# Attention and experts on one core: probabilities transposed in 32x32 blocks on VectorE, float32 products on eight tiles of the array, lists of tokens by comparisons

## The chip, the core and the metric

The kernel runs on one core of a Trainium2 chip. A core has a matrix engine (TensorE, PE in the profile; PEld is its loading of weights), a vector engine (VectorE, DVE), an engine for activations and copies (ScalarE, ACT), a general engine (GpSimd, POOL), and an engine that here only issues transfers (SyncE, SP). Each has its own queue of instructions, and semaphores hold an instruction until what it needs is there. Data live in HBM, in SBUF (128 partitions) and in PSUM, where the matrix engine writes (eight banks of 512 float32 a partition). The metric is the device time of one execution in microseconds.

## What is computed

Attention of 8 batches, each of 8 heads, 576 positions and 64 dimensions, with rotary positions; then a mixture of 8 experts over the 4608 tokens of 512 values, each token in the one expert that its gate puts first.

```python
q_rot, k_rot = (rotate(q), rotate(k))
scores = scale * np.matmul(q_rot, k_rot.transpose(0, 1, 3, 2))
scores = scores - np.max(scores, axis=-1, keepdims=True)
attn = np.exp(scores)
attn = attn / (np.sum(attn, axis=-1, keepdims=True) + 1e-09)
x = np.matmul(attn, v)                       # then [tokens, heads x dims]
...
logits = x @ w_gate
e_idx = np.argmax(logits, axis=1)            # gate_w: its softmax value
eom = 1.0 / (1.0 + np.exp(-(x @ w_output_gate)))
for e in range(E):
    mask = e_idx == e
    h = np.maximum(x[mask] @ w1[e], 0.0)     # 512 -> 1024
    out[mask] = gate_w[mask, None] * eom[mask, e, None] * (h @ w2[e])
```

## The kernel before

The attention runs over 32 pairs of heads (8 batches of 4 pairs), 9 steps a pair. A step is 128 queries of one head against all 576 keys; the middle one, step 4, holds the last 64 queries of both heads. `Attention.step` emits, for each step, the scores, the peak, the exponential, the transposes and the splits of earlier steps; a table of events (`CFG["events"]`) hangs all other work on a step number counted from the pair's first step, and may be negative (preparation) or over 8 (work that falls into the next pair's steps).

For precision, an operand is taken as a sum of two parts of 12 bits, each of the matrix engine's fast form of float32 (f32r). What happens to a pair:

- **Preparation.** One transfer brings q and k, already transposed and doubled for the rotation (L373). POOL multiplies (L383) and adds (L387), and makes the high part of k (L362) and the low parts of k, q and v (L368); ScalarE makes the high parts of q and v (L360). SP then stacks the high and low parts of one head on 128 partitions by transfers from SBUF to SBUF (`ks` L408, `qs` L427, `bd` L433).
- **Scores.** 4 products of 128x288 a step (L478), 6 at the middle step (L472), two PSUM banks a step, two steps in flight. VectorE takes the peak (L484), ScalarE the exponential with the row's sum (L496).
- **Transposes.** TensorE turns each step's probabilities in blocks of 128x128 (L517, and L535 and L538 for the last 64 keys): 41 a pair. ScalarE takes the high part out of PSUM (L457), VectorE the low one (L461).
- **Products with the values.** 40 a pair (L562), 320 or 256 columns, the result transposed. It is taken out by ScalarE or VectorE (L360, L362).
- **Back.** 10 float32 products a pair (L581, each two records in the trace) transpose it back, add the parts of v, and give the gates' logits; VectorE divides by the sums (L587, L589).

After a batch's fourth pair, `place` works out the gates and each token's place in the list of its expert: 18 small pieces, one a step, most on VectorE, and then five scatters of token numbers to a list in HBM (L691), issued by POOL. Each scatter writes the same list, and so waits until the one before has landed.

The experts take slots of 256 (or 128) tokens of one expert. POOL gathers the rows (L895), TensorE transposes them (L933), the first product (L961, L951) and the second (L989) follow, POOL scatters the result (L1001). All weights are split into two parts on ScalarE (L917) and VectorE or POOL (L919). The first slots use lists that are complete two batches before the end; the lists for the others need the last batch's scatters.

Of the kernel before, what the change touches and what calls it, by code (L numbers as in the profile page):

```python
# [20 lines left out]
NP = H // 2  # L21
# [7 lines left out]
XW = DM + 1  # L29
BIG = float(1 << 22)  # L30
SLOT = 256
CFG = {
    "L": 2, "LH": 2, "LL": 2, "order": "SP1TXH2L0", "trr": 5, "por": 5, "ra": "P", "rm": "P", "pm": 4, "pt": [2,
    1], "place": 18, "placek": 2, "kh": "P", "kl": "P", "qh": "A", "ql": "P", "vh": "A", "vl": "P", "dup": "A",
    "ac": "AVVV",
    "events": [
# [5 lines left out]
    ],  # L42
}

# columns of the table of constants
C_E8, C_MASK, C_TOK, C_EB, C_SL, C_II, C_TRI, C_ONE = range(8)
# [6 lines left out]
def slot_counts(nb):  # L53
    """Slots of 256 tokens of an expert that the first nb - 2 batches certainly fill; those that certainly get more than
    128 after these; and the most slots of 128 that the rest may need."""
    n0 = min(5, -(-((nb - 2) * S - E * (SLOT - 1)) // SLOT)) if nb > 2 else 0
    n0 = max(0, n0)
    T = nb * S - n0 * SLOT
    n2 = max(0, -(-(T - E * P) // SLOT))
    return n0, n2, (T + E * (P - 1)) // P - 2 * n2  # L60


def const_table(nb):
    """Constants that depend on the shapes alone: [128, n] float32, with the column ranges."""
    p = np.arange(P, dtype=np.float32)[:, None]
    ii = np.concatenate([np.eye(D), np.eye(D)], 0)
# [4 lines left out]
    mask[QR:, 2] = 0.0  # L71
    tok = p + 128.0 * np.array([0, 1, 4, 2, 3])[None, :]
    eb = np.tile(np.arange(E) * float(list_rows(nb)), (P, 1))
    sl = np.concatenate([p // 2, p], 1)
    parts = [e8, mask, tok, eb, sl, ii, tri, one]
# [4 lines left out]
def rope_table():  # L80
    """cos and signed sin, in the layout [pair of heads x D, 2, S]."""
# [9 lines left out]

def body(ctx, tc, nb, offs, qk, v, rope, cst, gates, w, out):
# [6 lines left out]
    # what lives to the end; what the preparation of a pair needs (right); what the rest of the attention needs  # L99
# [6 lines left out]
    ps_t = pool(ctx, "ps_t", 2, space=PSUM)  # L106
    ps_a = pool(ctx, "ps_a", 2, space=PSUM)
    ps_s = pool(scores, "ps_s", 2, space=PSUM)
    pools = px, px2, pa2, pp1, pp2, ps_s, ps_t, ps_a
    # the rows of x with their gates, and the list of each expert's tokens  # L110
    xd = dpool.tile([NT, XW], F32, name="xd")
    nl = E * list_rows(nb)
    lst = dpool.tile([nl, 1], F32, name="lst")
# [4 lines left out]
    o = offs[C_II]  # L118
# [3 lines left out]
    stage = pa2.tile([P, 2, S], F32, tag="pm", name="stage", bufs=CFG["pm"]).rearrange("p a b -> p (a b)")  # L122
# [3 lines left out]
    ii = cpool.tile([P, H, D + 16], F32, name="ii")  # L126
# [3 lines left out]
    zero, big = stage[:, nst:nst + 256], stage[:, nst + 256:nst + 256 + nl // P]  # L130
    nc.vector.memset(zero, 0.0)
    nc.vector.memset(big, BIG)
    nc.scalar.dma_start(out=ct, in_=cst[:, 0:o])
    nc.scalar.dma_start(out=stage[:, 0:nst], in_=cst[:, o:])
    nc.scalar.dma_start(out=ii[:, :, D:], in_=gates)

    def consts():
        nc.vector.tensor_copy(ii[:, :, 0:D], sc(C_II).unsqueeze(1).broadcast_to((P, H, D)))
        nc.vector.tensor_copy(trib, sc(C_TRI))
        nc.vector.tensor_copy(oneb, sc(C_ONE))  # L140
        nc.vector.memset(cnt, 0.0)
        nc.sync.dma_start(out=lst.rearrange("(p n) o -> p (n o)", p=P), in_=big)

    att = Attention(tc, nb, pools, cc, ident, ii, first, trib, oneb, cnt, zero, qk, v, xd, lst)
    n0 = slot_counts(nb)[0]
    moe = Moe(tc, nb, (px, px2, ps_t), cc, ident, cnt, w, xd, lst, out)
    # the first slots' tokens are known before the last two batches
    if n0:
        g = att.done(nb - 3) + 1
        for k, f in enumerate(pieces(moe.table0(), 14)):  # L150
            att.at(g + k, 2, f)
        att.at(att.done(nb - 2) - att.nplace + 22, 2, moe.fetch)
# [7 lines left out]
    for g in range(att.G, att.G + 4):  # L160
        att.step(g)
    scores.close()
    if not n0:
        att.rest(lambda g: True)
        main.close()
        moe.open_right(pool(ctx, "mr", 1, side="right", reuse_waits="tile"))
        left = []
    else:
        att.rest(lambda g: g <= att.G + 4)
        moe.begin1()  # L170
        att.rest(lambda g: True)
        main.close()
    moe.open_left(pool(ctx, "ml", 1, side="left", reuse_waits="tile"),
                  pool(ctx, "ps_m", 1, space=PSUM, reuse_waits="tile"))
    if n0:
        # the tables of the slots are worked out beside the scatters
        a, b, n = att.last, pieces(moe.table1(), 60), len(att.last) - 10
        left = a[:n] + [lambda f=f, g=g: (f(), g()) for f, g in zip(a[n:], b)] + b[10:]
# [9 lines left out]
def pieces(gen, n):  # L188
    """The (at most n) parts of a generator as functions, to be called in turn."""
# [3 lines left out]
class Attention:  # L193
    """The attention of all pairs of heads, emitted step by step."""

    def __init__(self, tc, nb, pools, cc, ident, ii, first, trib, oneb, cnt, zero, qk, v, xd, lst):
        nc = tc.nc
        px, px2, pa2, pp1, pp2, ps_s, ps_t, ps_a = pools
# [4 lines left out]
        def init(bd, z, rz, ac):  # L203
# [3 lines left out]
            nc.gpsimd.memset(ac[1][:, 2, QR:], 0.0)  # L207

        for i in range(2):
            o = (pp1.tile([P, 2, P], F32R, name=f"bd{i}"), px.tile([P, 2 * NCH], F32, name=f"z{i}"),  # L210
                 px.tile([P, 2 * NCH], F32, name=f"rz{i}"), [px.tile([P, NCH, P], F32, name=f"ac{h}_{i}") for h in range(2)])
            self.inits.append(lambda o=o: init(*o))
            own.append(o)
        lgp = px.tile([P, NCH, H, 16], F32, name="lgp")
        self.inits.append(lambda: nc.gpsimd.memset(lgp, 0.0))
# [6 lines left out]
        # pieces of work by the step (9 a pair) and the place in it at which they are emitted  # L222
# [5 lines left out]
        def newxb(b):  # L228
            xbs[b] = px2.tile([P, NCH, XW], F32, tag="xb", name=f"xb{b}")

        for n, pr in enumerate(self.pairs):
            g, b = 9 * n, n // NP
            fs = {"load": pr.load, "rot1": lambda pr=pr: pr.rot(1), "key": pr.key, "rot0": lambda pr=pr: pr.rot(0),
                  "query": pr.query, "loadv": pr.loadv, "value": pr.value, "den": pr.den,
                  "tr0": lambda pr=pr: pr.rem(0), "tr1": lambda pr=pr: pr.rem(1),
                  "lo0": lambda pr=pr: pr.remlow(0), "lo1": lambda pr=pr: pr.remlow(1)}
            for h in range(2):
                for a in range(2):
                    for k in range(2):
# [871 lines left out]
```

## Time and profile before

| what | value |
|---|---|
| time, median of 3 runs | 1231.0 us (1230.33 to 1232.42) |
| span of the profiled execution | 1253.2 us |
| first product of scores | at 15.0 us |
| last product with the values | at 717.8 us |
| last interval without a matrix product over 10 us | 793.2 to 823.3 us |
| first products of the experts | at 730.7 us |

The profiled execution's own time is not given apart from its span; the span is 1.8% above the median of the runs. In the lines below, a row of a timeline gives start, duration, engine, line, operation, output and inputs, shapes and count; "a group of a line" gives count, then busy time and the mean of one in ns, then the idle time of the engine before it. Matrix products overlap, so that the distance from start to start, not the duration, is what one of them takes.

### The profile page before, as it was taken

How to read it: one execution, taken by the hardware profiler on the slowest of the kernel's cores; microseconds unless marked ns; L12 is line 12 of the kernel's file. 1: busy time of each engine (PE TensorE's matmuls, PEld its weight loads, DVE VectorE, ACT ScalarE, POOL GpSimd, SP SyncE). 2: the span in 40 equal slices, each digit the busy share in tenths (PEclk: the TensorE clock that was granted, in tenths of full speed). 3: DMA queues.
4: the chain of work that ended last, by engine and by line, in shares of the span. 5: the costliest groups of instructions: out<-in, count | busy, mean ns of one | idle time of the engine just before them, and what ended most of it. 6: DMA issues, size and time to landing. Idle time of an engine off the chain costs nothing.

```text
span 1253.2 us, 22141 instructions
## 1 busy us (share of the span) xinstructions
PE 1094.3 (87%) x7603; PEld 1016.4 (81%) x7603; DVE 948.0 (76%) x1656; ACT 764.6 (61%) x1502; POOL 624.3 (50%) x412
## 2 busy tenths in 40 slices
PE   3999977988988869878888889379999999999997
PEld 2999877887978868868778889268898988989986
DVE  6899957978969859859789867246567776786784
ACT  3787755765756646746657654125467675776573
POOL 5777548567575575576475221122144363344242
PEclk9999988998988989999989989779999999999999
DMA  7866846847656756756756689757668878798791
GB/s 224 220 192 180 181 87 167 196 106 203 147 139 171 162 111 179 172 107 188 160 109 160 141 204 242 151 141 228 225 206 305 293 251 298 255 327 275 270 334 40
DMA packets 97395, 242.72 MB, mean 194 GB/s; under 512 B 27613, under 2 KB 28924, under 8 KB 93312
## 3 DMA queue, kind: packets, MB, share of 16 engines
q1 hardware_dynamic: 88032, 221.46, 64.1%
q0 software_dynamic: 7776, 18.94, 4.9%
q8 instruction: 64, 1.05, 0.4%
q10 hardware_dynamic: 1472, 0.85, 0.2%
q14 instruction: 51, 0.42, 0.1%
HBM read 168.66 MB, written 20.11 MB: 151 GB/s over the span
## 4 chain that ended last, share of the span: by engine, by line
PE 34%; POOL 25%; issue 22%; DMA 13%; DVE 2%; SPq 1%; ACT 1%; POOLq 0%; ACTq 0%; DVEq 0%
PE py L989 14%; POOL raw L383 11%; PE ph L961 11%; POOL raw L387 5%; PE ph L951 4%; DMA qs<-raw 3%; DMA lst<-tok,pi 3%; POOL raw L368 2%; POOL lst L691 2%; POOL kl L368 2%; DMA ks<-kh 2%; DMA xg<-xd,0idx 2%; PE mtp L933 1%; DMA ks<-kl 1%; POOL kh L362 1%
## 5 line engine op out<-in xcount | busy, mean ns | idle before, releaser
L919 DVE TENSOR_TENSOR wl<-wr,wh 128x1024 fp32r<-128x1024 f32 x183 | 254.3, 1402 | 51.6 <-ACT wh L917 50.2
L496 ACT ACTIVATE pm<-sc,m 128x576 f32<-128x576 f32 x288 | 214.8, 746 | 80.1 <-DVE m L484 75.3
L484 DVE TENSOR_REDUCE m<-sc 128x1 f32<-128x576 f32 x288 | 215.6, 749 | 60.0 <-PE sc L478 58.5
L478 PE MATMUL sc<-ks,qs 128*128 128x288 f32 x1024 | 202.8, 323 | 65.2 <-DMA qs<-raw 45.0
L457 ACT CAST pt<-tp 128x512 fp32r<-128x512 f32 x288 | 168.3, 584 | 128.1 <-PE tp L517 127.8
L461 DVE TENSOR_TENSOR pt<-tp,pt 128x512 fp32r<-128x512 f32 x288 | 196.8, 683 | 34.0 <-ACT pt L457 30.5
L478 PEld LDWEIGHTS sc<-ks,qs 128*128 128x128 f32 x1024 | 157.4, 201 | 79.5 <-issue 48.6
L917 ACT CAST wh<-wr 128x1024 fp32r<-128x1024 f32 x208 | 212.8, 1050 | 8.4 <-DMA wr<-in_w 8.4
L989 PE MATMUL py<-wh,ht 128*128 128x512 f32 x640 | 216.4, 403 | 0.0
L562 PE MATMUL acc<-pt,vs 128*128 128x256 f32 (+1 forms) x1024 | 192.2, 314 | 8.2 <-POOL vs L368 5.8
L517 PE MATMUL tp<-ident,pm 128*128 128x128 f32 x1152 | 183.2, 284 | 13.0 <-DVE pt L461 11.6
L383 POOL TENSOR_TENSOR raw<-raw,rt 128x1152 f32<-128x1152 f32 x62 | 164.2, 2649 | 10.0 <-DMA raw<-in_qk 8.6
L961 PE MATMUL ph<-xt,wh 128*128 128x256 f32 x896 | 161.6, 283 | 0.2 <-DVE ht L964 0.2
L517 PEld LDWEIGHTS tp<-ident,pm 128*128 128x128 f32 x1152 | 145.7, 147 | 17.7 <-DVE pt L461 11.6
L562 PEld LDWEIGHTS acc<-pt,vs 128*128 128x128 f32 x1024 | 148.8, 193 | 13.7 <-POOL vs L368 7.2
L989 PEld LDWEIGHTS py<-wh,ht 128*128 128x128 f32 x640 | 121.2, 189 | 25.0
L961 PEld LDWEIGHTS ph<-xt,wh 128*128 128x128 f32 x896 | 139.1, 190 | 1.8 <-DVE xt L936 0.6
L691 POOL DMA_INDIRECT lst<-tok,pi x40 | 41.5, 1036 | 198.1 <-DMA lst<-tok,pi 140.4
L989 PE MATMUL py<-wl,ht 128*128 128x512 f32 x320 | 126.2, 394 | 0.0
L961 PE MATMUL ph<-xt,wl 128*128 128x256 f32 x448 | 126.2, 282 | 0.0
L919 POOL TENSOR_TENSOR wl<-wr,wh 128x1024 fp32r<-128x1024 f32 x25 | 61.3, 2454 | 86.6 <-ACT wh L917 73.3
L581 PE MATMUL po<-ii,ac 128*128 128x80 f32 x640 | 86.3, 286 | 5.6 <-DVE lgp L589 5.6
(194 smaller groups left out, 1769.9 us busy)
## 6 DMA issues: line engine op xcount, KB each, us to landing
wr<-in_w SPq DMA_DIRECT2D x208, 512.0 KB, 5.3
raw<-in_qk SPq DMA_DIRECT2D x31, 1152.0 KB, 6.0
qs<-raw SPq DMA_DIRECT2D x124, 256.0 KB, 4.6
vraw<-in_v SPq DMA_DIRECT2D x32, 320.0 KB, 6.8
xd<-xb SPq DMA_DIRECT2D x16, 513.0 KB, 7.3
ks<-kh SPq DMA_DIRECT2D x32, 144.0 KB, 6.4
ks<-kl SPq DMA_DIRECT2D x32, 144.0 KB, 5.3
ks<-kh SPq DMA_DIRECT2D x32, 128.0 KB, 4.9
```

Source lines behind the costliest of these rows:

```text
L383: self.eng(eng).tensor_tensor(out=rv, in0=rv, in1=self.rt[:, 2 * t:2 * t + 2, x], op=ALU.mult)
L457: self.nc.scalar.copy(hi, src)
L461: self.nc.vector.tensor_tensor(out=lo, in0=src, in1=hi.bitcast(F32), op=ALU.subtract)
L478: nc.tensor.matmul(ps[:, a, :HS], self.qs[h][:, w, c * P:c * P + P], self.ks[h][:, a * HS:a * HS + HS], start=(w == 0), stop=(w == 1))
L484: nc.vector.tensor_reduce(self.m[i], ps[:, :, :HS], axis=AX.XY, op=ALU.max, negate=True)
L496: nc.scalar.activation(pe.rearrange("p (a b) -> p a b", a=2), self.ps[i][:, :, :HS], AF.Exp, bias=self.m[i], scale=1.0, accum_out=self.z[: ...
L517: nc.tensor.transpose(out=tp[:, k, :], in_=pe[:, k0 + k * P:k0 + k * P + P], identity=ident)
L562: nc.tensor.matmul(acc[:, 0:n], self.vs[:, 2 * k + h, :, :].rearrange("p a b -> p (a b)"), m, start=(i == 0), stop=(i == 9))
L917: self.nc.scalar.copy(wh, r)
L919: eng.tensor_tensor(out=wl, in0=r, in1=wh.bitcast(F32), op=ALU.subtract)
L961: nc.tensor.matmul(ph[:, f, :], st[:, dc, fs], mv[:, dc, :], start=(n == 0), stop=(n == 11))
L989: self.nc.tensor.matmul(py[h], st[:, f, hs], mv, start=(f == 0 and n == 0), stop=(f == 7 and n == 2))
```

## The change

**Scores.** The stacking transfers are gone. `kh`, `kl` and `q` stay as they are, the first head on partitions 0 to 63, the second on 64 to 127, and a step has 6 products over 64 rows instead of 4 over 128:

```diff
-            for w in range(2):
+            r = slice(h * D, h * D + D)
+            for n, (w, mov) in enumerate(((1, self.kh), (1, self.kl), (0, self.kh))):
                 for a in range(2):
-                    nc.tensor.matmul(ps[:, a, :HS], self.qs[h][:, w, c * P:c * P + P], self.ks[h][:, a * HS:a * HS + HS],
-                                     start=(w == 0), stop=(w == 1))
+                    nc.tensor.matmul(ps[:, a, :HS], self.q[r, w, c * P:c * P + P],
+                                     mov[r, a * HS:a * HS + HS], start=(n == 0), stop=(n == 2))
```

`bd` for the middle step is copied by ScalarE (`lasts`). High parts of k and q are made on ScalarE, low ones on POOL. q and k come in two transfers.

**Transposes.** One VectorE instruction turns the 32x32 blocks of a step's 128x576 probabilities, a step later, from SBUF to SBUF; the 41 transposes, the casts (L457) and the subtractions (L461) are gone:

```diff
+        self.nc.vector.transpose(out=self.pt[:, st[0] + 5 * st[1] if st else 4, :], in_=self.pc.pop(i))
```

**Products with the values.** After the block transposes, the 32 partitions `32a` hold 32 keys of block j for the queries whose number within a chunk lies in quarter a. So v is loaded four times, once on each 32 partitions (four transfers of 288 KB), and for each of 18 blocks of keys there are 8 float32 products of 32 rows by 64 columns of the array, one for each quarter of queries and each head, in one accumulator of four banks:

```diff
+        for a in range(4):
+            r = slice(32 * a, 32 * a + 32)
+            for h in range(2):
+                u, o, n = (0, 32, 4 + (a < 2)) if h == 0 else (5 - (a > 1), 32 - 32 * (a > 1), 4 + (a > 1))
+                nc.tensor.matmul(self.acc[h * D:h * D + D, a, o:o + 32 * n], self.v[r, h, j, :],
+                                 self.pt[r, u:u + n, 32 * j:32 * j + 32], start=(j == 0), stop=(j == NB - 1),
+                                 skip_group_check=True)
```

That is 144 products a pair (L503), emitted in four pieces of 40, 40, 32 and 32 at steps 12, 14, 16 and 17 (steps 3, 5, 7 and 8 of the next pair). Three copies on ScalarE take the result out, five float32 products of 160 columns (L518) at step 19 transpose it back into the same four banks, three VectorE and two ScalarE instructions divide.

On TensorE, at step 3 of the second pair, the order before has transposes and products between scores (tp: transposed probabilities in PSUM; acc: the accumulator; pt, vs: parts of probabilities and values):

```order
L517 MATMUL tp_5_8963<-ident,pm_2_8932 128x128 x4
L478 MATMUL sc_8_8971<-ks_31_8528,qs_31_8549 128x288 x4
L517 MATMUL tp_6_8978<-ident,pm_2_8932 128x128 x4
L562 MATMUL acc_31_8989<-pt_31_8805,vs_8851 128x320
L562 MATMUL acc_31_8989<-pt_31_8806,vs_8851 128x320
```

and now, with scores of one step, the piece of 40 begins:

```order
L463 MATMUL sc_3_327<-kh_181,q_213 128x288 x2
L463 MATMUL sc_3_327<-kl_182,q_213 128x288 x2
L463 MATMUL sc_3_327<-kh_181,q_213 128x288 x2
L503 MATMUL acc_338<-pt_140,v_232 64x160
L503 MATMUL acc_338<-pt_140,v_232 64x128
L503 MATMUL acc_338<-pt_140,v_232 64x160
L503 MATMUL acc_338<-pt_140,v_232 64x128 x2
L503 MATMUL acc_338<-pt_140,v_232 64x160
```

The full-size products (L562) of the order before are shown in the last pair, where a row of scores stands among them; the small ones now run without a score between for 40 in a row. Each of them is compiled to two loads of weights and two products on the same tile, one after the other, as each float32 product is.

**VectorE.** In steady steps before (m: the peak; pt: the low part; ac: taking out; xb, lgp: the division):

```order
L484 TENSOR_REDUCE m_3_6580<-sc_3_6575 128x1
L362 COPY ac_0_113<-acc_22_6582 128x256
L461 TENSOR_TENSOR pt_23_6547<-tp_1_6588,pt_23_6546 128x4x128
L362 COPY ac_0_112<-acc_22_6569 128x256
L484 TENSOR_REDUCE m_4_6619<-sc_4_6612 128x1
L461 TENSOR_TENSOR pt_23_6547<-tp_2_6621,pt_23_6546 128x4x128
```

and now:

```order
L469 TENSOR_REDUCE m_5_9426<-sc_5_9419 128x1
L484 STREAM_TRANSPOSE pt_9266<-pm_4_9411 128x576
L469 TENSOR_REDUCE m_6_9489<-sc_6_9482 128x1
L484 STREAM_TRANSPOSE pt_9266<-pm_5_9428 128x576
L781 CAST 0ri<-0row 128x1
L469 TENSOR_REDUCE m_7_9505<-sc_7_9498 128x1
```

The transpose of one step stands behind the peak of the next, where the subtraction stood behind a transpose of TensorE and a cast of ScalarE.

**Lists.** `place` has 38 pieces; its small operations are on POOL (on VectorE for the last batch). A token's place in the lists is split into a row and a column; VectorE compares row numbers (128x288, five times), POOL column numbers times the token's number (128x128, five times, L676), five products of 128x288 (L684) add both up to an array of all lists in SBUF, and it is written to HBM once for the first slots and once for the rest. No scatter is left on POOL:

```order
L691 DMA lst<-tok_1869,pi_1976 36864x1
L383 TENSOR_TENSOR raw_1998<-raw_1998,rt 128x1152
L387 TENSOR_TENSOR raw_1998<-raw_1998 128x576
L691 DMA lst<-tok_1869,pi_1976 36864x1
L383 TENSOR_TENSOR raw_1998<-raw_1998,rt 128x1152
```

is POOL's order of before, between the rotations of a pair (raw: q and k with their rotation); now the same engine has

```order
L412 TENSOR_TENSOR raw_4570<-raw_4570,rt 128x1152
L621 COPY xb_3004<-eg_4595 128x5
L416 TENSOR_TENSOR raw_4570<-raw_4570 128x576
L676 TENSOR_SCALAR pl_4909<-row,lo_4815,tok_4821 128x128 x2
L394 TENSOR_TENSOR kl_4935<-raw_4570,kh_4934 128x576
```

where the comparisons stand between the rotations, and wait for VectorE and POOL alone.

```diff
+        nc.vector.tensor_scalar(T["ro"][:, c, :], row, T["hr"][:, c:c + 1], 0.0, op0=ALU.is_equal, op1=ALU.add,
+                                accum_out=T["no"][:, c:c + 1])
+        nc.gpsimd.tensor_scalar(T["pl"][:, c, :], row[:, 0:P], T["lo"][:, c:c + 1], T["tok"][:, c:c + 1], op0=ALU.is_equal,
+                                op1=ALU.mult)
...
+            nc.tensor.matmul(T["ls"], T["pl"][0:m, c, :], T["ro"][0:m, c, :], start=(c == 0), stop=(c == 4), skip_group_check=True)
```

**The end of the attention.** The first slot's rows are transposed, and its first 48 products (L991) emitted, between the last piece of products with the values and the back products; the last batch's `place` runs beside the first slots, two pieces for each part of a slot.

```diff
+            att.rest(lambda g: g <= att.G + 1)
+            for u in range(3):
+                moe.split(u)
+            att.rest(lambda g: g <= att.G + 8)
+            for h in range(2):
+                moe.turn(0, h)
+            for j in range(2):
+                moe.products(0, j)
             att.rest(lambda g: True)
```

More of the change, by code (lines that the diff above doesn't have):

```diff
@@ L105, in body @@
     pp1, pp2 = pool(early, "pp", 1, side="right"), pool(early, "pp2", 2, side="right")
[L106 to L109, printed above, removed]
+    ps_a = pool(main, "ps_a", 1, space=PSUM, side="left")
+    ps_s = pool(scores, "ps_s", 2, space=PSUM, side="right")
+    small = Small(ps_s)
+    pools = px, px2, pa2, pp1, pp2, ps_s, small, ps_a
     xd = dpool.tile([NT, XW], F32, name="xd")
-    nl = E * list_rows(nb)
-    lst = dpool.tile([nl, 1], F32, name="lst")
+    nl = E * list_rows(nb) // P
+    lst = [dpool.tile([nl, P], F32, name=f"lst{c}") for c in range(2)]
     first = Pair.first(tc, pools, qk[0, 0], rope)
@@ L159, in body @@
         moe.begin0()
-    for g in range(att.G, att.G + 4):
+    for g in range(att.G, att.G + TURN):
         att.step(g)
     scores.close()
+    small.move(pool(ctx, "ps_x", 2, space=PSUM, side="right", reuse_waits="tile"))
+    moe.ph = pool(ctx, "ps_h", 1, space=PSUM, side="right", reuse_waits="tile")
     if not n0:
@@ L193, with __init__ @@
 class Attention:
-    def __init__(self, tc, nb, pools, cc, ident, ii, first, trib, oneb, cnt, zero, qk, v, xd, lst):
+    def __init__(self, tc, nb, pools, cc, ident, ii, first, trib, oneb, cnt, zero, qk, v, xd, row, lists):
         nc = tc.nc
-        px, px2, pa2, pp1, pp2, ps_s, ps_t, ps_a = pools
+        px, px2, pa2, pp1, pp2, ps_s, small, ps_a = pools
         NT = nb * S
@@ L246, in __init__ @@
+            for name, o, k in EVENTS:
+                if n > 1 or name not in ("load1", "load0", "mult1", "add1", "kh", "kl", "mult0", "add0", "qh", "ql")[:10 if n == 0 else 2]:
+                    at(g + (3 if name == "lasts" and n == 0 else o), k, fs[name])
             if n % NP == NP - 1:
-                fs = place(tc, (px, px2, ps_t, ps_a), b, NT, cc, trib, oneb, cnt, lgp, xbs, xd, lst)
-                self.nplace = len(fs)
+                fs = place(tc, (px, px2, small), self.pairs, b, NT, cc, trib, oneb, cnt, xbs, xd, row, lists)
@@ L595, in place, with number @@
+def number(NT, b):
+    m = NT // S // 2 * S
+    return float(b * S - m + (b * S >= m))
+def place(tc, pools, pairs, b, NT, cc, trib, oneb, cnt, xbs, xd, row, lists):
     nc = tc.nc
-    p1, p2, ps_t, ps_a = pools
-    V = nc.vector
+    p1, p2, small = pools
+    last = b == NT // S - 1
+    V = nc.vector if last else nc.gpsimd
     tt = V.tensor_tensor
@@ L600, in place, with new @@
     T = {}
[L602 to L603 removed]
+    def new(n, sh, dt=F32, **k):
+        T[n] = p2.tile(sh, dt, tag=n, name=f"{n}{b}", **k)
         return T[n]
@@ L781, in slots, with turned @@
         V.tensor_copy(idx, tr[:, 0, 0:m])
+    def turned(self, k):
+        nc, N = self.nc, self.lists.shape[1]
+        tr, lt = self.small.tile(f"ltr{k}"), self.t([P, -(-N // P), P], f"lt{k}")
+        d = self.rowsd = self.lst[k]
+        for g in range(0, N, P):
+            nc.tensor.transpose(out=tr[0:min(P, N - g), g // P, :], in_=self.lists[:, g:min(N, g + P)], identity=self.ident)
+        yield
+        n, m = N // P, N % P
+        if n:
+            nc.scalar.copy(lt[:, 0:n, :], tr[:, 0:n, :])
+            nc.scalar.dma_start(out=d[0:n * P, :].rearrange("(g p) c -> p g c", p=P), in_=lt[:, 0:n, :])
+        if m:
+            nc.scalar.copy(lt[0:m, n, :], tr[0:m, n, :])
+            nc.scalar.dma_start(out=d[n * P:N, :], in_=lt[0:m, n, :])
+        yield
     def starts(self, n, g, last):
@@ L930, in turn @@
         xth, xtl = self.xt[s]
-        tp = self.ps_t.tile([P, 4, P], F32, tag="tp", name=f"mtp{s}_{h}{self.nm}")
+        tp = self.small.tile(f"mtp{s}_{h}{self.nm}")
         for dc in range(4):
```

539 lines of the change are left out of this document (251 added, 288 removed), and 8 rows, old and new, of tables (CFG, EVENTS).

## The prediction

> **What bounds the kernel now.** I read the page's totals and its chain first, then busy time in stretches, then the timeline of each engine inside one stretch. The page:
>
> ```profile
> span 1253.2 us, 22141 instructions
> ...
> PE 1094.3 (87%) x7603; PEld 1016.4 (81%) x7603; DVE 948.0 (76%) x1656; ACT 764.6 (61%) x1502; POOL 624.3 (50%) x412
> ...
> PE 34%; POOL 25%; issue 22%; DMA 13%; DVE 2%; SPq 1%; ACT 1%; POOLq 0%; ACTq 0%; DVEq 0%
> ```
>
> TensorE is busiest, yet POOL and time in "issue" hold nearly half of the chain. The stretches say why (columns: length, then busy time of PE, PEld, DVE, ACT, POOL, clock, DMA share, GB/s):
>
> ```profile
> 46.10:63.10 17.00, 17.00 (x142) 17.00 (x141) 15.39 (x31) 14.20 (x34) 13.09 (x8) 1.00 0.76 209
> 182.30:271.70 89.40, 76.33 (x559) 72.05 (x559) 73.67 (x149) 57.49 (x135) 57.25 (x37) 0.94 0.64 158
> 900.00:1240.00 340.00, 337.18 (x2209) 305.10 (x2208) 249.52 (x264) 226.04 (x328) 137.42 (x78) 1.00 0.77 268
> ```
>
> The first is one pair of heads with nothing of the gates beside it: 17.0 us, PE never idle. The second is four pairs with a batch's lists beside them: 22.4 us a pair, PE idle for 13 of 89 us. The third is the experts, PE idle for 3 of 340 us; nothing there is touched but the first slot. The middle step's first product marks each pair, so its first and last row give the mean period:
>
> ```profile
> 27.41 0.37 PE L472 MATMUL sc<-kh,bd 128*128 128x288 f32 x1 [0.62 <-issue]
> ...
> 702.46 0.43 PE L472 MATMUL sc<-kh,bd 128*128 128x288 f32 x2
> ```
>
> 31 periods in 675.05 us are **21.8 us each**, 4.8 above the pure PE time. The waits name the culprit: POOL stands at a scatter until the one before has landed, and the next pair's rotation is queued behind it.
>
> ```profile
> POOL lst L691 <- DMA lst<-tok,pi: 140.4, 23, 11.3
> ...
> PE sc L478 <- DMA qs<-raw: 45.0, 11, 15.0
> ```
>
> So two things can be won: the 4.8 us of stall in each pair, and whatever the new pair takes below 17.0.
>
> **The change, per pair: TensorE.** Prices come from start-to-start distances in the timeline, since matmuls overlap (the last row is of the chain in order of time):
>
> ```profile
> 97.13 0.43 PE L472 MATMUL sc<-kh,bd 128*128 128x288 f32 x2
> 97.39 0.42 PE L472 MATMUL sc<-kl,bd 128*128 128x288 f32 x2
> 97.66 0.43 PE L472 MATMUL sc<-kh,bd 128*128 128x288 f32 x2
> 97.92 0.60 PE L517 MATMUL tp<-ident,pm 128*128 128x128 f32 x4
> 98.28 0.78 PE L478 MATMUL sc<-ks,qs 128*128 128x288 f32 x4
> ...
> 102.50 1.01 PE L581 MATMUL po<-ii,ac 128*128 128x80 f32 x8
> 103.35 0.60 PE L517 MATMUL tp<-ident,pm 128*128 128x128 f32 x4
> ...
> 853.13 2.77 PE py L989 x12
> ```
>
> A score product of 288 columns takes 0.79/6 = 0.132 us, a float32 record of the back product 0.85/8 = 0.106, an expert product of 512 columns 2.77/12 = 0.231, that is 0.45 ns a column. The change removes 41 transposes a pair (0.36/4 = 0.09 each or a little more, about 4 us), all 40 halved products, and 10 of 20 back records. It raises the scores from 38 to 54 products: 54 x 0.132 = 7.1 us. Five back products (10 records of 160 columns) are taken at 0.14: 1.4 us.
>
> The unknown is V, the time of the new 144 float32 products, 288 records on eight tiles. No row shows a tile of the array, so I bound V. If a record streams its 144 columns (mean of 160 and 128) twice, it needs 288 x 0.45 = 0.13 us. All eight tiles filled: 288 x 0.13 / 8 = 4.7 us. One record after another: 37 us. In between stands the back record: with only 80 columns moving it still takes 0.106, more than 160 x 0.45 = 0.072, so I read it as paced by its 128 weight columns. Half as many columns would give 0.053, in series 288 x 0.053 = 15.3 us, and with the left and right column halves loading side by side 7.6. **I take V = 8**, as the row nearest in kind is the weight-paced one; the ends 4.7 and 37 stay. V stands in four pieces between scores, and each change between full and tiled products may drain the array: a 288-column product lasts 0.29 (0.42 for two 0.13 apart) but costs 0.13, so a drain is 0 to 0.16; some 12 changes give 0 to 1.9 us, taken as 0.5.
>
> **VectorE.**
>
> ```profile
> 9.68 0.76 DVE L368 TENSOR_TENSOR kl<-raw,kh 128x576 fp32r<-128x576 f32 x1
> 10.36 0.42 DVE L387 TENSOR_TENSOR raw<-raw 128x256 f32<-128x256 f32 x1
> ...
> 67.25 0.55 DVE L587 TENSOR_TENSOR xb<-po,rz 128x384 f32<-128x384 f32 x1
> 67.71 0.25 DVE L589 TENSOR_TENSOR lgp<-po,rz 128x96 f32<-128x96 f32 x1
> ...
> 74.49 0.68 DVE L461 TENSOR_TENSOR pt<-tp,pt 128x512 fp32r<-128x512 f32 x1
> 75.09 0.75 DVE L484 TENSOR_REDUCE m<-sc 128x1 f32<-128x576 f32 x1
> 75.75 0.16 DVE L548 TENSOR_SCALAR rz<-z 128x10 f32<-128x10 f32 x1
> ```
>
> The peak costs 75.75 - 75.09 = 0.66. The block transpose has no row; a 576-column operation from SBUF to SBUF costs 10.36 - 9.68 = 0.68, and I take that (nothing excludes half of it, which would take 1 us off the pair by the three steps below, nor twice, which would put VectorE at 20.8 us and above PE). Nine of both are 12.1 us; the division adds about 1.1 (0.46 + 0.16 for three of five chunks), the denominators 0.5, the comparisons and sums of the lists about 1: **14.7 us**, a floor for the pair, or 1.63 a step. It replaces the 0.60 subtraction, so VectorE gains little and loses little.
>
> **ScalarE, POOL, DMA** stay below that floor.
>
> ```profile
> L496 ACT ACTIVATE pm<-sc,m 128x576 f32<-128x576 f32 x288 | 214.8, 746 | 80.1 <-DVE m L484 75.3
> ...
> L496 ACT ACTIVATION_READ_ACCUMULATOR pm<-sc,m 128x1 f32 x288 | 57.1, 198 | 0.0
> ...
> L383 POOL TENSOR_TENSOR raw<-raw,rt 128x1152 f32<-128x1152 f32 x62 | 164.2, 2649 | 10.0 <-DMA raw<-in_qk 8.6
> L387 POOL TENSOR_TENSOR raw<-raw 128x576 f32<-128x576 f32 x62 | 88.3, 1424 | 4.9
> ```
>
> ScalarE: 9 x (0.746 + 0.198) = 8.5, and about 3.3 for kh, qh, bd, eviction and the last chunk. POOL: 2 x 2.65 + 4 x 1.42 = 11.0, and some 2 for the small operations of the lists, which now sit in its queue ahead of the rotation but wait for no landing. DMA moves 1152 KB of q and k and four times 288 KB of v, 2.3 MB, 11 us at the 209 GB/s of the first stretch; the stacking transfers, which the scores waited for, are gone, and SP's loads no longer stand behind them.
>
> **One wait is new**: there is a single accumulator, so the first products wait for the division of the pair before, and the next scores stand behind them in PE's queue. The order puts two steps between, 3.2 us at VectorE's pace, against a division of 1.1; I cost it at nothing, and up to 1 us a pair if that cover is gone.
>
> **The pair.** Six of nine steps carry V beside their scores (0.79 a step: 6 x 0.132): 4.7 + 8 + 0.5 = 13.2 us, paced by PE. The other three go at VectorE's pace, two operations and the division, about 1.93 a step: 5.8. Together **19.0 us**. That is slower than the 17.0 of an undisturbed pair: the gain is the stall that goes, 21.8 - 19.0 = 2.8 us, times 31 = **87 us**.
>
> **The ends.**
>
> ```profile
> 15.03 1.30 PE L478 MATMUL sc<-ks,qs 128*128 128x288 f32 x4 [15.03 <-DMA qs<-raw]
> ...
> 717.41 0.40 PE L562 MATMUL acc<-pr,vs 128*128 128x256 f32 x2
> ...
> 726.54 4.39 PE L581 MATMUL po<-ii,ac 128*128 128x80 f32 x20
> 730.67 0.77 PE L961 MATMUL ph<-xt,wh 128*128 128x256 f32 x2
> ...
> 823.26 1.11 PE L933 MATMUL mtp<-ident,xg 128*128 128x128 f32 x4 [30.04 <-DMA xg<-xd,0idx]
> ...
> 824.38 4.66 PE py L989 x12
> ```
>
> The first score waits for stacked queries: without them 2 us earlier. (The last row is again of the chain.) Between the last attention product and the first expert product lie 12.9 us; now 48 expert products stand there, and about 11 go (the back products remain). The 30.0 us of idling at 823 is a gather queued on POOL behind the last scatters, and 4.66 - 2.77 = 1.9 follow of slow restart; without scatters both go, 31 in all. That is 44 us. If the gather is still late, up to 31 of it stays.
>
> **Sum**, against the profiled execution's span: 1253.2 - 44 - 87 = 1122. The median shown, 1231.0, is 0.982 of that span, the only time shown for this execution; so 1122 x 0.982 = **1102 us**.
>
> **Rivals.** *Products in order (slower).* The compiled order puts a product's two records on the same tile next to each other. If records must start in the order written, the second waits for the first, and no more than two tiles run at once: V = 288 x 0.13 / 2 = 18 or more. PE alone then has 18 + 7.1 + 1.4 = 26.5 us a pair, and 29 if VectorE's three steps stay as above. At 26.5: 1253.2 - 44 + 31 x 4.7 = 1355, by 0.982 **1331 us** (1407 at 29). With weights loaded one at a time (V = 15.3) the same two forms give 23.8 and 26.3, that is 1248 to 1325. It decides from a pair of 21.8 + 44/31 = 23.2, with V = 12 in the form of the forecast. For it: no row shows two products of this array at once. Against: each tile is its own quarter of rows and half of columns. The Trainium skill, "TensorE: Matmul & The Clock Gate", Part 3: Packing small matmuls, speaks against the change here: matmuls start and end strictly in program order, and a weight load passes a running matmul only in another row group. The same section has 16 tiles at 10.6 times one, by which V would stay near 5; no run yet shows which holds for paired records.
>
> *VectorE and POOL in each other's way.* A VectorE operation beside POOL can be held:
>
> ```profile
> 8.86 0.68 DVE L383 TENSOR_TENSOR raw<-raw,rt 128x512 f32<-128x512 f32 x1
> ...
> 11.59 3.23 DVE L383 TENSOR_TENSOR raw<-raw,rt 128x640 f32<-128x640 f32 x1
> ```
>
> Beside POOL's rotation the second took 3.2 us instead of some 0.8. If each transpose is held by half of a POOL operation of 1.4 (0.65), 9 x 0.65 = 5.9 are added, VectorE needs 20.6, and the pair 21: 1253.2 - 44 - 25 = 1184, **1163 us**. Against: subtractions with one operand in SBUF kept to 0.68 with POOL 77% busy in the first stretch. The Trainium skill, "SBUF — State Buffer", Who interferes with whom, agrees: one SBUF input outside the two-port modes does not contend; by it this rival falls.
>
> *VectorE alone is the bound.* With V at 4.7 the pair lies between VectorE's 14.7 and 4.7 + 4.7 + 0.5 + 5.8 = 15.7, say 15.5: 1253.2 - 44 - 195 = 1014, **996 us**.
>
> *The gap stays.* If the lists of the last batch come no earlier, 31 us return: **1133**.
>
> **How the numbers follow.** Forecast with its own spread, 1060 to 1150 (the kept gap in it): 0.42. VectorE the bound, 980 to 1060: 0.17. Contention, 1150 to 1225: 0.12. Products in order or weights in series, 1240 to 1400: 0.25, half of it above 1290. Near 1231: 0.04. Leaving out what lies below 1000 (0.06) and above 1290 (0.13) gives 1000 to 1290. Faster by over 0.2% (what a measurement can tell) 0.71, the same 0.04, slower 0.25.
>
> **What would show it.** L503's busy stretch per pair near 8 us and a period near 19; four expert pieces without a gap after them; no wait of POOL on a list's landing. Records of L503 that start 0.13 us apart or more would prove the first rival; transposes above 1 us beside POOL the second; L503 at 5 with VectorE never idle the third. Wrong it is above all if V is.

## The result, and the profile after

The changed kernel takes **1155.9 us** (median of 5 runs, 1144.5 to 1157.9) where the kernel before takes 1231.0 (1228.5 to 1232.4): a ratio of 0.937, 95% interval 0.932 to 0.941. The forecast was 1102, the range 1000 to 1290: the gain is 75 us where 129 were forecast.

The page of the profiled execution (span and instructions; busy time; the chain that ended last; transfers of instructions), which was the shortest of the five executions:

```profile
span 1142.6 us, 34814 instructions
...
PE 1035.1 (91%) x14465; PEld 896.3 (78%) x14465; DVE 848.2 (74%) x1492; ACT 638.7 (56%) x1313; POOL 582.9 (51%) x539
...
q8 instruction: 115, 1.88, 0.7%
...
PE 66%; DVE 15%; issue 6%; POOL 5%; ACT 5%; DMA 2%; SPq 0%; POOLq 0%; ACTq 0%; DVEq 0%
```

POOL's share of the chain went from 25% to 5%, "issue" from 22% to 6%, and TensorE carries two thirds of it. There are twice as many matrix records, and 1.88 MB of instructions where it was 1.05.

The stretches (length; busy PE, PEld, DVE, ACT, POOL; clock; DMA) of an undisturbed pair, of four pairs with the lists, of the attention between the first and the last middle step, of the part from there up to the first expert product after the 48 early ones, and of the rest:

```profile
60.66:76.69 16.03, 15.42 (x357) 12.80 (x353) 13.91 (x27) 10.38 (x28) 10.84 (x6) 1.00 0.51 150
340.70:415.50 74.80, 67.67 (x1417) 56.83 (x1415) 59.81 (x125) 41.60 (x111) 52.59 (x56) 0.91 0.54 145
24.06:591.08 567.02, 513.62 (x10742) 429.35 (x10742) 465.04 (x960) 321.20 (x847) 388.10 (x396) 0.94 0.53 145
591.08:641.83 50.75, 35.51 (x612) 28.72 (x609) 21.37 (x47) 14.95 (x31) 10.74 (x17) 0.81 0.47 148
641.83:1142.00 500.17, 479.23 (x3092) 432.80 (x3092) 346.44 (x469) 294.25 (x421) 172.59 (x110) 0.98 0.72 246
```

31 periods in 567.0 us are 18.3 each, where they were 21.8: the attention gave 108 us. The same two last stretches of the kernel before are

```profile
702.46:730.67 28.21, 20.77 (x146) 19.66 (x144) 17.61 (x34) 15.38 (x31) 8.78 (x8) 0.86 0.92 204
730.67:1253.00 522.33, 483.20 (x3134) 435.96 (x3133) 348.03 (x454) 296.95 (x422) 175.17 (x109) 0.97 0.74 238
```

550.5 us there, 550.9 now: **from the last middle step on nothing was gained**, although the 30 us of waiting at 823 us are gone.

TensorE inside the undisturbed pair (start, duration, engine, line, names, shapes, count):

```profile
63.06 1.64 PE L503 MATMUL acc<-pt,v 32*64 32x160 f32 x80
64.63 0.53 PE L463 MATMUL sc<-kh,q 64*128 64x288 f32 x2
...
65.98 1.37 PE L503 MATMUL acc<-pt,v 32*64 32x160 f32 x64
...
68.44 1.37 PE L503 MATMUL acc<-pt,v 32*64 32x160 f32 x64
69.74 0.53 PE L463 MATMUL sc<-kh,q 64*128 64x288 f32 x2
...
71.28 1.77 PE L518 MATMUL acc<-ii,ac 128*128 128x160 f32 x10
72.98 0.53 PE L463 MATMUL sc<-kh,q 64*128 64x288 f32 x2
```

A piece of 80 records takes 1.57 us up to the next score, one of 64 takes 1.30 (the third piece has 0.1 of waiting in it). The difference is 16 records in 0.27 us, 17 ns each: 288 of them are 4.9 us, plus 0.2 a piece: 5.7 together. Back takes 1.70. What is left of the 15.4 busy us, 8.0, are the 54 scores.

What TensorE waited for in the whole run, and the longest such waits (the number behind the bracket is the idle time just before the row):

```profile
PEld acc L503 <- issue: 38.2, 110, 2.6
...
PE acc L503 <- issue: 17.8, 10, 2.4
PE sc L463 <- ACT pm L478: 15.9, 24, 1.8
...
PE acc L503 <- DVE cnt L649: 12.2, 6, 2.1
```

```profile
432.05 2.97 PE L503 MATMUL acc<-pt,v 32*64 32x160 f32 x80 [2.07 <-DVE cnt L649]
...
612.31 3.01 PE L503 MATMUL acc<-pt,v 32*64 32x160 f32 x147 [1.74 <-ACT xb L535]
615.54 0.84 PE L503 MATMUL acc<-pt,v 32*64 32x128 f32 x29 [0.21 <-issue]
617.61 0.56 PE L503 MATMUL acc<-pt,v 32*64 32x160 f32 x9 [1.23 <-issue]
620.52 4.01 PE L503 MATMUL acc<-pt,v 32*64 32x128 f32 x103 [2.35 <-issue]
...
641.83 0.77 PE L991 MATMUL ph<-xt,wh 128*128 128x256 f32 x2 [5.81 <-DVE ht L1009]
...
721.92 0.29 PE L797 MATMUL 2tr<-ident,2tk 18*128 18x18 f32 x1 [3.77 <-DVE 2tk L793]
```

The reader is to see three things. Seven batches have a wait of 2 us ahead of a piece of products, six of these put down to `cnt`, a sum of the lists that lies in the products' accumulator, and six have a second one of 2.3 us, which the trace puts down to issue. Behind nine of these 13 waits the clock is at a half: the 80 records of the row at 432.05 take 2.97 us instead of 1.64, at a granted clock of 0.50. The last pair's 288 records, with no scores between, take 12.2 us instead of 5. And the experts now begin with a wait for VectorE.

### The profile page after: what moved, and what is told of

The parts are those of the page before. It is cut to its first block, busy times and chain, and to the rows that moved or that the text cites. A ratio compares the mean times of both kernels' runs of the same rounds, so it can differ in the third digit from the quotient of the medians.

```text
span 1142.6 us, 34814 instructions
## 1 busy us (share of the span) xinstructions
PE 1035.1 (91%) x14465; PEld 896.3 (78%) x14465; DVE 848.2 (74%) x1492; ACT 638.7 (56%) x1313; POOL 582.9 (51%) x539
## 3 DMA queue, kind: packets, MB, share of 16 engines
q8 instruction: 115, 1.88, 0.7%
## 4 chain that ended last, share of the span: by engine, by line
PE 66%; DVE 15%; issue 6%; POOL 5%; ACT 5%; DMA 2%; SPq 0%; POOLq 0%; ACTq 0%; DVEq 0%
PE py L1034 17%; PE ph L991 14%; PE acc L503 13%; PE sc L463 11%; DVE m L469 4%; DVE pt L484 4%; PE ph L983 4%; POOL raw L412 3%; ACT pm L478 3%; PE sc L456 2%; PE mtp L969 2%; DVE xb L526 1%; PE acc L518 1%; DVE wl L955 1%; DMA v<-in_v 1%
## 5 line engine op out<-in xcount | busy, mean ns | idle before, releaser
L503 PE MATMUL acc<-pt,v 32*64 32x160 f32 (+1 forms) x9216 | 219.6, 318 | 40.6 <-issue 17.8
L463 PE MATMUL sc<-kh,q 64*128 64x288 f32 x1024 | 220.6, 329 | 31.0 <-ACT pm L478 15.9
L503 PEld LDWEIGHTS acc<-pt,v 32*64 32x64 f32 x9216 | 176.4, 142 | 67.0 <-issue 38.2
L484 DVE STREAM_TRANSPOSE pt<-pm 128x576 f32<-128x576 f32 x288 | 220.6, 766 | 1.2 <-ACT pm L478 0.3
L463 PEld LDWEIGHTS sc<-kh,q 64*128 64x128 f32 x1024 | 149.9, 194 | 70.9 <-ACT pm L478 30.9
L991 PE MATMUL ph<-xt,wh 128*128 128x256 f32 x896 | 165.3, 287 | 7.0 <-DVE ht L1009 5.8
L991 PEld LDWEIGHTS ph<-xt,wh 128*128 128x128 f32 x896 | 142.8, 195 | 9.1 <-issue 6.0
L991 PE MATMUL ph<-xt,wl 128*128 128x256 f32 x448 | 128.1, 286 | 0.0
L463 PE MATMUL sc<-kl,q 64*128 64x288 f32 x512 | 111.2, 301 | 0.0
L394 POOL TENSOR_TENSOR kl<-raw,kh 128x576 fp32r<-128x576 f32 x31 | 43.7, 1409 | 91.6 <-ACT kh L386 91.5
L416 POOL TENSOR_TENSOR raw<-raw 128x576 f32<-128x576 f32 x62 | 88.2, 1422 | 3.0
L991 PEld LDWEIGHTS ph<-xt,wl 128*128 128x128 f32 x448 | 87.8, 196 | 0.0
L463 PEld LDWEIGHTS sc<-kl,q 64*128 64x128 f32 x512 | 85.7, 195 | 0.0
```

What stands on the lines that cost most here:

```text
L416: self.eng(eng).tensor_tensor(out=r[:, 2 * t, x], in0=r[:, 2 * t, x], in1=r[:, 2 * t + 1, x], op=ALU.add)
L463: nc.tensor.matmul(ps[:, a, :HS], self.q[r, w, c * P:c * P + P], mov[r, a * HS:a * HS + HS], start=(n == 0), stop=(n == 2))
L484: self.nc.vector.transpose(out=self.pt[:, st[0] + 5 * st[1] if st else 4, :], in_=self.pc.pop(i))
L503: nc.tensor.matmul(self.acc[h * D:h * D + D, a, o:o + 32 * n], self.v[r, h, j, :], self.pt[r, u:u + n, 32 * j:32 * j + 32], start=(j == 0) ...
L991: nc.tensor.matmul(ph[:, f, :], st[:, dc, fs], mv[:, dc, :], start=(n == 0), stop=(n == 11))
```

## The experiments

### The changed kernel again, twice

> The changed kernel again, to see what differs between its executions (1144 and 1155 to 1158 us so far). If the spread is the granted clock alone, a slower execution shows the same stretches of work, stretched where the clock is at a half, and no new wait. The rival: the slower executions have a wait of their own, as a late transfer. Median expected within 1 us of 1156.

> The changed kernel once more, beside the next two on the same chip, as what they are measured against: a ratio to the kernel before between 0.92 and 0.94.

| run | median us | before, same chip | ratio (95%) |
|---|---|---|---|
| first again | 1150.1 | 1244.7 | 0.922 (0.917 to 0.927) |
| second again | 1154.5 | 1233.5 | 0.936 (0.932 to 0.940) |

Chips differ by 1% for the kernel before, so edits below are held against runs on their own chip where there is one. The first repetition was expected within 1 us of 1156 and took 1150.1, on another chip. TensorE's idle time in the attention is the same (53.2 us, and 53.4 above), so no new wait shows there. From the first to the last middle step the first repetition took 578.7 us (third stretch above: 567.0) at a mean clock of 0.92 (0.94), and the part behind them 546.6 (550.9): in the attention, the executions differ by how long the clock is at a half (525.5 busy us for the same records, against 513.6).

### The same products in another order

```diff
-    def values(self, j):
+    def values(self, b0, b1):
...
         for a in range(4):
             for h in range(2):
+                for j in range(b0, b1):
```

> The 144 products in another order: within a piece all blocks of keys of one tile, then the next tile, five or four products of a tile in a row where they were eight tiles in turn. Theory A (products begin in the order written): a tile's records follow one another at 0.11 to 0.14 us, neighbours overlap only at the seams, so the 288 records take 20 to 37 us where they take 5, and the undisturbed pair goes from 16 to over 30 us, the time over 1600 us. Theory B (the engine looks far ahead and fills free tiles): the products stay under 8 us and the time within 60 us of the changed kernel.

2431.8 us (one run). One tile's first six records, a piece later in the same pair, and that pair's stretch:

```profile
213.48 1.02 PE L504 MATMUL acc<-pt,v 32*64 32x160 f32 x6 [0.31 <-ACT xb L536]
...
226.31 13.26 PE L504 MATMUL acc<-pt,v 32*64 32x160 f32 x80
```

```profile
222.80:280.50 57.70, 57.70 (x354) 51.31 (x353) 15.36 (x28) 10.49 (x27) 10.98 (x7) 0.53 0.15 42
```

Six records end after 1.02 us and one lasts about 0.3, so that they start some 0.14 apart; the piece of 80 takes 13.3 us against 1.57, at half clock (6.6 at full). Theory A holds for the price: the same work on the same tiles costs four times as much at equal clock, eight as it ran, when a tile's products follow one another. (That products begin strictly in the order written does not hold; see the last section.) TensorE is then busy without a break, yet its clock is at 0.53, which neither theory had.

### Every transpose twice

```diff
+        for _ in range(2):
             self.nc.vector.transpose(out=self.pt[...], in_=pe)
```

> Every block transpose is done twice, into the same place: nine more VectorE operations of some 0.68 us a pair, 6.1 us. Theory (TensorE paces the undisturbed pair of 16.0 us, VectorE is busy for 13.9 of it): the first 2.1 us are hidden, the undisturbed pair takes 20 to 20.5 us and the time is 110 to 140 us above the changed kernel. Rival 1 (VectorE and POOL hold each other up): transposes of over 0.8 us and a pair above 22. Rival 2 (VectorE has far more slack): under 18.

1296.3 us (one run), 142 above the changed kernel on that chip, where up to 140 were expected. The undisturbed pair, 20.7 us where up to 20.5 were expected:

```profile
92.10:112.80 20.70, 18.00 (x355) 14.78 (x352) 20.29 (x36) 10.35 (x27) 10.77 (x7) 0.91 0.42 116
```

VectorE has no slack left (20.3 of 20.7 us), and 9 x 0.68 on 13.9 gives 20.0: a transpose costs 0.68, and the pair had 2.1 us of cover. Neither rival holds; in the changed kernel all 288 transposes last 714 to 779 ns, with POOL busy for half of the span:

```profile
L484 DVE STREAM_TRANSPOSE pt<-pm x288: 714/767/779, 19.4 to 608.0; 128x576 f32<-128x576 f32 x144
```

### The lists' sums read at once

```diff
-    17: lambda: (s14(), s9()), 18: s14b, ... 35: s20, 36: s21
+    17: lambda: (s14(), s14b(), s9()), ... 35: lambda: (s20(), s21())
```

> The sums of the lists that lie in the accumulator (ranks, and the lists themselves) are read out by VectorE in the step in which TensorE forms them, not one step later. Theory (the new wait for the one accumulator is what the lists cost): the 14 waits of 2.1 to 2.3 us before the next products go to under 0.4, 26 us, and of the some 60 us at half clock that follow such waits in the attention most go too, 15 to 30 us; together 40 to 55 us, 1100 to 1115. Rival (POOL's small operations are the bound, and the wait moves on to the scores): under 10 us. Second rival (the clock falls whatever the waits): 26 us alone.

1123.1 us, ratio 0.899 (0.893 to 0.904), against 1150.1 and 0.922 on the same chip: 27 us, where 40 to 55 were expected. TensorE's waits, first of the changed kernel there, then of this one:

```profile
PE acc L503 <- issue: 16.1, 9, 2.3
PE sc L463 <- ACT pm L478: 16.0, 24, 1.8
...
PE acc L503 <- DVE cnt L649: 10.2, 5, 2.1
...
PE acc L503 <- ACT xb L535: 7.8, 16, 1.7
```

```profile
PE sc L463 <- ACT pm L478: 26.8, 35, 1.8
...
PE acc L503 <- ACT xb L535: 13.8, 24, 1.7
...
PE acc L503 <- issue: 4.6, 3, 2.9
```

and their attention, first to last middle step:

```profile
23.70:602.40 578.70, 525.51 (x10741) 439.04 (x10741) 465.52 (x960) 321.37 (x847) 388.14 (x396) 0.92 0.52 142
```

```profile
23.80:576.90 553.10, 505.20 (x10742) 419.26 (x10742) 462.82 (x956) 321.00 (x845) 387.88 (x396) 0.96 0.54 148
```

The waits for `cnt` are gone, and so are the six of 2.3 us put down to issue: these too came from the lists in the accumulator. The clock rose from 0.92 to 0.96. In these two executions the attention is 25.6 us shorter. Idle time of TensorE (length less busy) fell from 53.2 to 47.9, only 5 us, since other waits grew: those of the scores by 10.8, those for the division (`xb`) by 6.0. Its busy time, for the same number of records, fell by 20: that is the clock. The execution profiled here is the longest of its five, and its part behind the last middle step is 8 us longer (555.1 against 546.9), so that the two profiles differ by 17 us where the medians differ by 27. The theory named the place, but the gain is half to two thirds of what it asked for. The size is that of the second rival, 26 us; its mechanism, a clock that stays, is not what happened. What moved on to the scores is what the first rival had foreseen.

### The weights held back

The first eight weight loads are made to wait for a small ScalarE copy that stands behind the last products. The edit also moves the first three splits of weights behind these products.

> The experts' first eight weight loads (512 KB each) wait until the last pair's products are done; nothing else is changed. Theory (TensorE's instructions come by the same transfers as the weights, and the last pair's 576 loads and products in a row run dry behind them): the stalls of 1 to 2.4 us that the trace puts down to issue among the last products, and the slow piece of 5.9 us before them, go; from the last middle step to the last product with the values it takes 25 to 28 us instead of 33, while the first expert product comes later, since its weights do: the time within 8 us of the changed kernel, either way. Rival (the last products are slow because of the half clock alone): the stalls stay with the transfers quiet.

```profile
612.77 1.37 PE L503 MATMUL acc<-pt,v 32*64 32x160 f32 x64
615.40 1.77 PE L518 MATMUL acc<-ii,ac 128*128 128x160 f32 x10 [1.27 <-ACT ac L512]
618.92 3.48 PE L503 MATMUL acc<-pt,v 32*64 32x160 f32 x185 [1.74 <-ACT xb L535]
622.90 2.13 PE L503 MATMUL acc<-pt,v 32*64 32x128 f32 x103 [0.50 <-issue]
```

The 288 records take 6.1 us (618.92 to 625.03) instead of 12.2, and one stall of 0.5 us is left. Their stretch in the changed kernel, here, and in a later run that holds the second four loads:

```profile
612.31:624.46 12.15, 8.35 (x288) 7.05 (x289) 5.31 (x12) 2.78 (x3) 0.00 (x0) 0.76 1.02 303
```

```profile
618.92:625.03 6.11, 5.61 (x289) 5.09 (x290) 1.72 (x8) 0.00 (x0) 0.00 (x0) 1.00 0.03 7
```

```profile
595.29:602.60 7.31, 7.31 (x289) 7.08 (x290) 5.31 (x12) 2.78 (x3) 0.00 (x0) 0.70 0.03 6
```

Two things differ from the changed kernel. Without the transfers (DMA share 0.03 instead of 1.02) idle time fell from 3.8 us to 0.5, and in the later run to nothing. And the clock was 1.00 instead of 0.76, so that busy time fell from 8.4 us to 5.6; in the later run, at 0.70, it is 7.3 with no stall at all. Of the 6 us, then, some 3.3 are stalls and 2.7 the clock: the theory and its rival each have a part. From the last score to the last product it is 12.2 us (22.8 from the last middle step, less than was expected); in ten executions with the loads beside it 15.0 to 20.4, 18.3 in the changed kernel's. The slow piece of 5.9 us is gone too, but it is not in the first repetition either (2.8 us), and what makes it stays open. So the stalls come with the weights' transfers; that it is the instructions that come late fits the word "issue" and the 16 KB blocks of the instruction queue (1.88 MB in 115), but is inferred. The weights are then late: TensorE waits 10 us for the first slot's rows, whose copy on ScalarE stands behind the splits of these weights. The time is 1159.8 us, 0.940 (0.935 to 0.945), 19 above the next run on that chip: more than the 8 that were expected.

### The early expert products put back

```diff
+        att.rest(lambda g: True)
         for h in range(2):
             moe.turn(0, h)
         for j in range(2):
             moe.products(0, j)
-        att.rest(lambda g: True)
```

> The first slot's transposes and its 48 first products are emitted behind the last back products again, not ahead of them. Theory (they fill a wait that is there anyway, for the copies out of the accumulator): 2 to 4 us slower, since the 48 products and the transposes, 8 us, then stand in a row behind a division of 1.1 us and a copy of 1 us. Rival (they are of no use, since the next part waits for VectorE in any case): within 1 us.

1140.8 us, 0.926 (0.921 to 0.932); no changed kernel ran on this chip beside it, so the runs of the changed kernel (0.922 to 0.937) leave open whether that is a gain. The trace is clearer: from the last product with the values to the 49th expert product it takes 14.6 us, in three executions of the changed kernel 17.2 to 17.3. (From the last middle step it is 42.3 against 45.7 to 50.8, but the rest of that difference lies ahead of the edit, in the last pair's products.) The theory falls: having the products early gains nothing, and by this one execution costs some 2.7 us.

### The relu ahead of the splits

`first(0, 0)` and `first(0, 1)` are called ahead of the next three splits of weights.

> The two relu steps of the first 48 products stand ahead of the next three splits of weights on ScalarE and VectorE. Theory: the 5.8 us in which TensorE waits at 636 us for the relu shrink to under 1.5, and the half clock of 7 to 10 us behind them goes: 5 to 9 us faster. Rival (the splits are late instead, and the second products wait as long): no gain.

1143.1 us, 0.926 (0.921 to 0.932), within the noise of the run before it, on the chip without a changed kernel. The wait of 5.81 us became 2.97, and from the last product with the values to the 49th expert product it takes 14.4 us instead of 17.3. But the rest, up to the end, takes 504.2 us where three executions of the changed kernel have 500.8 to 501.4: a wait of 2.1 us for the last batch's ranks came further on. In the trace the 5 to 9 us do not appear, as the rival had it.

### The index later

```diff
-            yield from self.slots(2, ..., 2, 5)
+            yield from self.slots(2, ..., 2, 7)
```

> In the tables of the last slots the transposed token numbers are asked for one part of a slot later (two more places between the gather of the list and its use). Theory: TensorE's two waits of 3.8 us at 718 and 748 go, and the half clock of 10 and 3 us behind them: 8 to 14 us. Rival (the list itself arrives late, and the first product that needs its rows waits as long): no gain.

1143.6 us, 0.918 (0.913 to 0.924), beside 0.922 (0.917 to 0.927): not told apart. The waits were 3.77 and 2.33 instead of 3.77 twice. Late is VectorE, which corrects the numbers just ahead of the transpose, behind a split of weights: in the changed kernel the correction begins at 720.89 us, as the split ends, and the transpose waits until 721.92. The edit had moved both.

### Three edits, and a fourth

Sums at once, relu first, and two places between the correction and the transpose; then also the second four weight loads held.

> Three edits at once: the sums read at once, the relu first, and two more places between the corrected list of tokens and its transpose (the place that the run with a later index had left as it was). If each wait is its own: 27 us of the first, 5 to 9 of the second, and 7.5 us of waits with some 4 of half clock of the third, together 40 to 48 us under the changed kernel on the same chip (1150 gives 1102 to 1110). Rival (one limit behind all three, as VectorE): no better than the first edit alone.

> The kernel with three edits (sums read at once, relu first, corrected tokens two places ahead of their transpose) beside the changed kernel on the same chip: 30 to 45 us below it, ratio to the kernel before 0.89 to 0.905.

> The three edits, and the second four of the experts' weight loads wait until the last products with the values are done (the first four go ahead as they did). If the instructions of the last products run dry behind these transfers, the last products end 2 to 4 us earlier and so does the kernel, 2 to 4 us below the kernel with three edits. Rival (the weights are then late for the first slot's second half): no gain, or up to 5 us slower.

| kernel | median us | ratio to before (95%) |
|---|---|---|
| three edits, first chip | 1110.6 | 0.900 (0.894 to 0.907) |
| changed, second chip | 1154.5 | 0.936 (0.932 to 0.940) |
| three edits, second chip | 1116.3 | 0.905 (0.902 to 0.908) |
| and weights held, second chip | 1118.1 | 0.906 (0.903 to 0.909) |

The three edits are worth **38 us** on top of the change (second chip) and beat both kernels; on the first chip there was no changed kernel to hold them against. The rival, that they are no better than the first edit alone, is not excluded by the times: that edit has 0.899 on a third chip, and no chip ran both. The traces speak against it. With the three edits the stretch from the 49th expert product on, with 0.9 and 0.5 us left of the two waits for the index, is

```profile
613.30:1106.00 492.70, 474.86 (x3092) 428.48 (x3092) 349.01 (x471) 296.85 (x423) 175.32 (x110) 0.99 0.72 250
```

It is 492.9 in the execution on the first chip; the changed kernel's three, to the end of their spans, have 500.8 to 501.4, and the first edit alone 504.1. Holding the later weights gained nothing, as its rival had it: the last 288 records ran without a stall (7.3 us, where the two executions with three edits took 8.1 and 8.9), but the ranks of the last batch then kept TensorE waiting for 5.5 us, where it had been 2.0.

## Why the prediction was right, and where not

- **The whole.** The time lies in the range, but by luck: not in the forecast's own spread (1060 to 1150), but in the one given to contention of VectorE and POOL, which did not happen. The attention gave more than was forecast, the ends almost nothing.
- **What bound the kernel.** Right in kind: the stalls behind the scatters. POOL's part of the chain fell to 5% and the attention's period by 3.5 us. But this was to be 2.8: the whole stall of 4.8 gone, and an undisturbed pair slower by 2.0. By the stretches the stall (mean period less undisturbed pair) fell from 4.8 to 2.3, and the undisturbed pair from 17.0 to 16.0. No run puts back the scatters, the transposes on TensorE or the stacked operands alone, so what each part of the change gave is read from the stretches and not shown.
- **V, the products.** The mechanism at the lower end was right and the value too large: 4.9 us and 0.8 for four changes of piece, where 8 and 0.5 were taken. On one tile a record takes 0.109 (128 columns) to 0.136 us (160) in the run by tiles, an eighth of which is 14 to 17 ns: all eight tiles were filled. The back record is no guide: a tile's weights are loaded while the other seven work.
- **Products in order.** The rival fell for this order (17 ns a record), but not its idea: the run by tiles shows what a row of records on one tile costs. What it had wrong is that the two records of a float32 product, next to each other, would block the tiles behind them. They do not.
- **Scores and back.** 8.0 and 1.7 where 7.1 and 1.4 were summed; six products behind a piece take longer, the first two start 0.37 apart from the next pair of products, not 0.26.
- **VectorE, POOL.** 0.68 for a transpose held (0.68 to 0.70 from start to start), and so did "no contention", as the Trainium skill, "SBUF — State Buffer", Who interferes with whom, has it for one input in SBUF outside the two-port modes.
- **The pair.** 16.0 us undisturbed, but 18.3 on the mean against 19.0. That these are near is luck, errors with opposite signs: V with its changes was 2.8 too dear, and three steps at VectorE's pace were to add 2.0 to TensorE's own time, where 0.6 of idling is measured; scores and back were 1.2 too cheap; and the lists, priced at 1 us of VectorE under cover, go with the 2.3 between the undisturbed pair and the mean. The rival with VectorE alone had a pair of 15.5, but at 13.9 us VectorE is not what paces these 16.0. The step "one wait is new", costed at nothing, missed that the lists use the same accumulator; the run that reads them at once shows 27 us for it, mostly as clock. That is some 0.9 of the 2.3 a pair; the rest is not taken apart here.
- **The ends.** This is the step that failed. Of the 44 us, the 2 at the start came (the first middle step is 3.3 us earlier), the other 42 did not. The gap at 823 did go, 32 with its slow restart (30.0 and 1.9, added up to 31 in the forecast), and came back in three places. The boundary: 28.2 us before, 50.8 now, of which 5.9 are the 48 expert products done early (the first slot's transposes stood in it before too), so 17 more; the 11 us forecast there as a gain were a loss, as the last pair's 288 records stand alone behind its scores and run dry (6 us by the run with held weights, stalls and clock together). In the two repetitions the boundary is 45.7 and 50.6. Then the wait for the relu (5.8, inside the boundary). Then, behind the first 48 products, 500.2 where 522.3 - 31.9 - 5.9 = 484.5 was to be expected: two waits of 3.8 for the index, and 13 us of work at half clock behind them and behind the relu's wait, which cost 6.4. What I priced was the wait that ended last; I did not ask what would be late next on VectorE.
- **The scale.** The sum of 1122 us for the span stands against 1142.6: the ends cost 41 more, the attention gave 21 more. The factor 0.982 made it 1102, but the profiled execution after was 1.2% under its median, not 1.8% above. So 20 us of the miss are the sum, and 34 the assumption that profile and median stand to each other as before. After the change that ratio is chance, of an execution's clock: 0.953 in the one profiled, 0.940 to 0.944 in the four of 1155 to 1158 us. For the kernel before it stays open; its profiled execution is longer than all five of its timed ones.

## What to carry to other kernels

Small products paid here on tiles of the array only when neighbours in the order sat on different tiles: interleave the tiles, and count a tile's record once for eight of them. When a long wait is removed, price what stands behind it on every engine, and look for a resource that two parts now share, as the accumulator here. Where many small instructions run without a break beside large transfers, look for stalls of "issue" (3.8 us in the last 12 of the attention here); holding the transfers back took the stalls away but no time, since the weights were then late.

## What the runs showed of the hardware

- Eight tiles take a record each within 0.05 us (the first eight start from 63.059 to 63.106 us), with both records of each float32 product next to each other in the kernel's order:

```profile
63.06 0.39 PE L503 MATMUL acc<-pt,v 32*64 32x160 f32 x8
```

  The weights of the second tile, on the same rows as the first, began to load at 63.064 us, with the first tile's record under way.

  The Trainium skill, "TensorE: Matmul & The Clock Gate", Part 3: Packing small matmuls, has products start strictly in program order. In the run by tiles that does not hold across tiles: the second tile's first record starts at 214.355 us, the first tile's eighth, ahead of it in the order, at 214.485. Some three records seem to wait at a tile before those of the next are let through.
- The clock fell to a half behind nine of the changed kernel's 13 waits of 2 us, for 3.4 to 10.2 us, and not behind the four others. It was there too with TensorE busy for 57.7 of 57.7 us on one or two tiles at a time (0.53). What sets it is not settled here.
